# A ConvNeXt V2 block on one core: the normalised block on three of every four partitions, read in three parts, and written from ScalarE's queue

## The chip, the cores and the metric

The kernel runs on one core of a Trainium2 chip. The metric is the device time of one execution in microseconds; the comparison is between medians of several runs. A core has five engines that follow their own lists of instructions and meet only at semaphores: TensorE (PE, with weight loads shown apart as PEld), VectorE (DVE), ScalarE (ACT), GpSimd (POOL) and SyncE (SP), which here only issues DMAs. The data are moved by 16 DMA engines, which all queues share.

## The reference, cut to what matters

```python
def reference(x, dw, w1, w2, grn_gamma, grn_beta):      # x: (1, 512, 512, 96), bf16
    xp = jnp.pad(x, ((0,0),(1,1),(1,1),(0,0)))
    out = jnp.zeros_like(x)
    for i in range(3):
        for j in range(3):                               # depthwise 3x3
            out = out + xp[:, i:i+H, j:j+W, :] * dw[i, j]
    h = _layernorm(out, axis=-1)                         # over the 96 channels
    h = jnp.einsum('bhwc,ce->bhwe', h, w1)               # 96 -> 384
    h = _gelu(h)                                         # tanh approximation
    gx = jnp.sqrt((h * h).sum(axis=(1, 2), keepdims=True) + 1e-6)   # over all pixels
    nx = gx / (gx.mean(axis=-1, keepdims=True) + 1e-6)
    h = grn_gamma * (h * nx) + grn_beta + h
    h = jnp.einsum('bhwe,ec->bhwc', h, w2)               # 384 -> 96
    return x + h
```

The sum over all pixels in `gx` divides the work: nothing of the output can be made before every pixel has gone through the first product and the GELU.

## The kernel before

The image is cut into 128 blocks of GR = 4 rows (2048 pixels x 96 channels). There are two passes.

**First pass (to about 980 us).** A loop over slots `s` (L826 to L949) works as a software pipeline: in one slot, different blocks stand at different stages. A table `at`, made ahead of the loop (L794 to L820), says which block has which stage in which slot. For a block b in the usual case:

- x is loaded (SP) and turned by VectorE; PE makes the convolution in three bursts of matmuls; ScalarE copies the result to SBUF as `y_bf` (`evac`).
- POOL squares it (`ysq`, L512), PE sums `y_bf` and `ysq` over channels, and for every four blocks VectorE and POOL make the reciprocal standard deviations. They go through DRAM: `stage_rows` (L608) writes them as rows, `stage_bcast` (L626) reads them back as four broadcasts onto 32 partitions each, as `rbc`.
- POOL multiplies: `yn` = `y_bf` x `rbc` (`stage_norm`, L634), three buffers. The mean needs no step: the matrix w1 is centred instead (`setup_mlp`, L425).
- One slot later `stage_write` (L642) writes `yn` to `yn_dram` with four DMAs of 96 KB, one per row of the block (SBUF has four image rows of 32 channel groups on its 128 partitions; DRAM has one row per channel). One slot after that `stage_read` (L647) reads the block back as `ynT`, 96 channels on partitions 0 to 95, with one DMA of 384 KB, into a ring of six buffers. Partitions 96 to 127 of the ring were filled with zeros once (`setup_ynt`), and so were rows 96 to 127 of `w1p`, since the matmuls contract over 128 partitions.
- Two slots later the block has its "mlp" stage (`mlp_units`, L699): PE multiplies `ynT` and `w1p` into PSUM banks, and ScalarE makes the GELU, in nine activations: three over two banks (1024 columns), six over one (512). VectorE takes statistics of the result, or PE its Gram matrix. A third of the blocks ("whole") keep the GELU's result: it is stored to `g_dram` in three DMAs, one per slot (`store_next`).

In a slot with an mlp stage of a block below TAIL0 = 114 the order on ScalarE is: GELU over banks 0-1, GELU 2, GELU 3, GELU 4-5, GELU 6, GELU 7, `evac` of the convolution, GELU 8-9, GELU 10, GELU 11. Slots of the last 14 blocks have an order of their own (`mlp_tail`).

**Order on the queues.** Every engine call of the pass goes through a wrapper that keeps it in program order on its engine. On SP a slot issues in this order: the x load of block s + 4, the read, the four writes, the broadcasts, the rows, the store of `g`. ScalarE's queue issues six small loads at the start of the kernel and nothing afterwards.

**Completion semaphores.** The framework gives the DMAs issued from SP's and ScalarE's queues eight completion semaphores, in turn and in the order of the built program. A DMA is issued only when the one that used its semaphore before, the eighth before it, has landed. The program holds this wait as an instruction of the issuing queue, so it holds up what stands behind it there. POOL's DMAs have their own eight.

**Second pass (from about 980 us).** After the statistics have been joined and w2 scaled, the blocks are gone through once more, in an order `ORDER` that mixes those whose GELU was kept (5 in SBUF, 35 in `g_dram`, loaded by POOL's queue) with those that are made again (88). For these, `load_rest` (L283) reads `ynT` five blocks ahead: 85 blocks by one DMA of 128 rows (`yn_rows`, L125: the 96 channel rows of the block and 32 of the next one, 512 KB; rows 96 to 127 of `w1p` are zero), while three are still in the ring. PE multiplies again, ScalarE makes the GELU over 1536 columns (`gr`), PE multiplies by w2, VectorE adds `xb` (x plus bias, made by POOL from `xr`, which POOL's queue loads) into `o_sb` (four buffers), and SP stores it (`stage_out`, L350), 384 KB per block.

The prediction speaks of the functions shown here.

Of the kernel before, what the change touches and what calls it, by code (L numbers as in the profile page):

```python
# [12 lines left out]
GR = 4  # L13
# [43 lines left out]
def kernel(  # L57
# [11 lines left out]
    f32 = mybir.dt.float32  # L69
# [40 lines left out]
    def chans(i):  # L110
        return slice(i, 64, 2) if i < 2 else slice(64, 96)
# [8 lines left out]
        return flat_ap.rearrange("p (g r m) -> p g r m", r=GR, m=MB)  # L120

    def yn_src(q):
        return yn_dram[q].rearrange("c (r w) -> c r w", r=GR)

    def yn_rows(q):  # L125
        return yn_dram[q:q + 2].rearrange("q c (r w) -> (q c) r w", r=GR)[0:128]

    def yn_dst(q, r):
        return yn_dram[q].rearrange("(c i) (r w) -> r c i w", i=NI, r=GR)[r]
# [6 lines left out]
    dwx = consts.tile([9, NI, GR, 32], bf16, name="dwx")  # L136
    eye32 = consts.tile([128, 32], bf16, name="eye32")
    rowsel = consts.tile([128, GR], bf16, name="rowsel")
    w1_raw = consts.tile([C, E], bf16, name="w1_raw")
    w1p = consts.tile([128, E], bf16, name="w1p")  # L140
    Wq = consts.tile([128, NI, 3, GR, 32], bf16, name="Wq")
    w2_sb = consts.tile([128, NCH, C], bf16, name="w2_sb")
# [41 lines left out]
    with ExitStack() as p1:  # L184
# [66 lines left out]
        for q in range(GR):  # L251
            dve.tensor_copy(out=eye32[32 * q:32 * q + 32, :], in_=ident_f[32 * q:32 * q + 32, 32 * q:32 * q + 32])

        cen = consts.tile([C, 128], bf16, name="cen")
        xtpool = pc.enter_context(tc.tile_pool(name="xt", side="right", bufs=1))
        ypool = pc.enter_context(tc.tile_pool(name="ybf", side="right", bufs=13))
        ysqpool = pc.enter_context(tc.tile_pool(name="ysq", side="right", bufs=3))
# [25 lines left out]
        def load_rest(n, sq, pq):  # L283
            q = ORDER[n]
            v = grp.setdefault(q, {})
            if is_held(q):
                v["g"] = gs[q]
            elif is_whole(q):
                v["g"] = late.gl.tile([128, NQ, NCH, QW], bf16, name="gl")
                pq.dma_start(out=v["g"][:].rearrange("p t j w -> p (t j w)"), in_=g_dram[whole.index(q)])  # L290
            else:
                ynt = yn_ring[SLOTS[nth_made[q] % NYT]]
                if q not in KEPT:
                    sq.dma_start(out=ynt[:], in_=yn_rows(q))
                v["ynt"] = ynt

        def recompute(q, t):
# [87 lines left out]
        for j in range(GR):  # L385
            pool.memset(rowsel[32 * j:32 * j + 32, j:j + 1], 1.0)
        pool.memset(cen[:], 1.0)
        pool.memset(w1p[C:128, :], 0.0)
        dve.memset(SG, 0.0)
        busy(FILL[0])  # L390
        Ud = banks(2)[:, 0, :NI * 9].rearrange("p (i k) -> p i k", i=NI)
# [7 lines left out]
        n = 0  # L399
# [12 lines left out]
                            pool.tensor_copy(out=o, in_=i_)  # L412

        for i in range(NI):
            act.dma_start(out=w1_raw[i:C:NI, :], in_=w1[chans(i), :])
        act.dma_start(out=w2_sb[:], in_=w2.rearrange("(j p) c -> p j c", p=128))
        with nc.allow_non_contiguous_dma("tiny gamma/beta load"):
            act.dma_start(out=gam_bf[:], in_=grn_gamma.rearrange("(j p) -> p j", p=128))
# [1 line left out]

        def setup_ynt():
            for t in yn_ring:
                pool.memset(t[C:128, :, :].rearrange("p r w -> p (r w)").bitcast(f32), 0.0)

        def setup_mlp():  # L425
            Us = banks(1)[:, 0, :]
            w1m, b2_ps = Us[:, :E], Us[:, E:E + C]
            pe.matmul(w1m, lhsT=cen[:], rhs=w1_raw[:], start=True, stop=True)
            for j in range(NCH):
                pe.matmul(b2_ps, lhsT=bet_bf[:, j:j + 1].to_broadcast([128, 128]), rhs=w2_sb[:, j, :],  # L430
                          start=(j == 0), stop=(j == NCH - 1))
            dve.scalar_tensor_tensor(out=w1p[:C, :], in0=w1m[:C], scalar=-1.0 / C, in1=w1_raw[:],
                                     op0=ALU.mult, op1=ALU.add)
            dve.tensor_copy(out=B2bc_f[:], in_=b2_ps)

# [203 lines left out]
                               in1=rbcs[k][:, b - b0:b - b0 + 1, :].to_broadcast([128, NI, W]), op=ALU.mult)  # L639
            yns[b] = yn  # L640

        def stage_write(b):  # L642
            yn = yns.pop(b)
            for r in range(GR):
                sp.dma_start(out=yn_dst(b, r), in_=yn[32 * r:32 * r + 32, :, :])

        def stage_read(b):  # L647
            t = yn_ring[b % NYT]
            sp.dma_start(out=t[:C], in_=yn_src(b))
            ynts[b] = t  # L650

        bsts = {}
# [173 lines left out]
        for s in range(last_slot + 1):  # L826
            get = lambda kind: at.get((s, kind), [])
            if s + 4 < NBLK:
                load_x(s + 4)
            for b in get("read"):  # L830
                stage_read(b)
            for b in get("write"):
                stage_write(b)
            for k in get("bcast"):
                stage_bcast(k)
            for k in get("rows"):
                stage_rows(k)
            store_next()
            for k in get("newton"):
                stage_newton(k, pool)  # L840
            for b in get("norm"):
                stage_norm(b)
            for b in get("sqp"):
                stage_sq(b, False)
            for k in get("rstd"):
                stage_rstd(k, pool)
            mlp = get("mlp")

            def spread_out():
                for k in get("spread"):  # L850
                    stage_spread(k)
                for b in get("norma"):
                    stage_norm(b, dve if b < 2 else pool)

            spare = not mlp and s % 2 == 1
            taps, evac = conv_taps(s, spare) if s < NBLK else ([], None)
            if mlp and mlp[0] >= TAIL0:
                assert not taps
                square_owed()
                mlp_tail(mlp[0], get)  # L860
            elif not mlp:
                if s + 3 < NBLK:
                    turn_x(s + 3)
                for f in taps:
                    f()
                if not spare:
                    spread_out()
                if evac:
                    evac()
                for b in get("sqa"):  # L870
                    stage_sq(b, True)
                for b in get("stats"):
                    stage_stats(b)
                for k in get("moments"):
                    stage_moments(k)
                if spare:
                    spread_out()
                for k in get("chain"):
                    stage_moments(k)
                    stage_chain(k)  # L880
                for k in get("turn"):
                    stage_turn(k)
                gram_next(2)
                square_owed()
            else:
                b = mlp[0]
                unit, squares, squares_rest = mlp_units(b)
                conv = lambda n, fence=True: taps[n](fence) if taps else None

                conv(0)  # L890
                unit(0, 2)
                unit(2, 1)
                squares(0)
                conv(1, False)
                spread_out()
                if s + 3 < NBLK:
                    turn_x(s + 3)
                unit(3, 1)
                unit(4, 2)
                squares(1)  # L900
                gram_next(1 if taps else 2)
                unit(6, 1)
                squares(2)
                unit(7, 1)
                for k in get("turn"):
                    stage_turn(k)
                conv(2)
                if evac:
                    evac()
                gram_next(1 if taps else 2)  # L910
                unit(8, 2)
                unit(10, 1)
                for b2 in get("stats"):
                    stage_stats(b2)
                unit(11, 1)
                for k in get("moments"):
                    stage_moments(k)
                squares_rest(2)
                square_owed()
                if is_whole(b):  # L920
                    owed.append(lambda f=squares_rest: f(3))
                grams.extend((b, c) for c in range(cm_quads(b) * QC, NQ * QC, 2 * E))
                if is_whole(b):
                    stores.extend((b, h) for h in range(3))
            if s == 0:
                setup_ynt()
            if s == 3:
                setup_mlp()
            if s == 4:
                setup_rest()  # L930
            for b in get("combine"):
# [120 lines left out]
```

## Time and profile before

| What | Value |
|---|---|
| Runs | 1480.27, 1486.15 and 1486.81 us; median 1486.15 |
| Profiled execution | span 1480.8 us from the first to the last instruction; granted TensorE clock 0.994 |
| Busy share of the span | ACT 96%, PE 94%, POOL 88%, DVE 80%, PEld 55% |
| DMA | 433 MB moved, 292 GB/s on average; SP's queue 326 MB, POOL's 103 MB |
| Writes of yn | 512 DMAs of 96 KB |
| Reads of ynT | 128 DMAs of 384 KB (first pass), 85 of 512 KB (second pass) |
| Stores of the output | 127 DMAs of 384 KB and 4 of 96 KB |

The time of the profiled execution is not listed beside its span; the span lies at the lower end of the runs. Busy times are sums over instructions, and an instruction that issues a DMA or waits for a semaphore is not counted as busy (on POOL, whose own cores prepare its DMAs, it is). The profile shows each wait with the engine or DMA that ended it; where a wait is for several things, it names the one that came last, and the names of DMAs in it can be off where several share a semaphore.

### The profile page before, as it was taken

How to read it: one execution, taken by the hardware profiler on the slowest of the kernel's cores; microseconds unless marked ns; L12 is line 12 of the kernel's file. 1: busy time of each engine (PE TensorE's matmuls, PEld its weight loads, DVE VectorE, ACT ScalarE, POOL GpSimd, SP SyncE). 2: the span in 40 equal slices, each digit the busy share in tenths (PEclk: the TensorE clock that was granted, in tenths of full speed). 3: DMA queues.
4: the chain of work that ended last, by engine and by line, in shares of the span. 5: the costliest groups of instructions: out<-in, count | busy, mean ns of one | idle time of the engine just before them, and what ended most of it. 6: DMA issues, size and time to landing. Idle time of an engine off the chain costs nothing.

```text
span 1480.8 us, 54225 instructions
## 1 busy us (share of the span) xinstructions
PE 1391.3 (94%) x23125; PEld 810.4 (55%) x23125; DVE 1182.0 (80%) x2135; ACT 1414.4 (96%) x1595; POOL 1300.3 (88%) x922
## 2 busy tenths in 40 slices
PE   8888999999999999999999997789999999999998
PEld 3434444444444444444444445467777777776776
DVE  7849989999999999999999987965555555555555
ACT  7888989999999999999999999999999999999997
POOL 3459889998998999998999987569999999999997
PEclk9999999999999999999999999999999999999999
DMA  5568788788888888888888866669999999999997
GB/s 180 179 205 255 241 253 280 228 271 260 260 248 264 258 264 255 276 253 254 263 258 266 263 216 195 195 225 409 366 359 402 417 416 413 419 410 417 411 412 282
DMA packets 167768, 433.08 MB, mean 292 GB/s; under 512 B 31558, under 2 KB 81318, under 8 KB 163046
## 3 DMA queue, kind: packets, MB, share of 16 engines
q1 hardware_dynamic: 151284, 326.04, 66.3%
q0 software_dynamic: 14880, 103.43, 17.6%
q8 instruction: 181, 2.97, 0.8%
q14 instruction: 61, 0.50, 0.1%
q10 hardware_dynamic: 1362, 0.15, 0.1%
HBM read 273.30 MB, written 156.22 MB: 290 GB/s over the span
## 4 chain that ended last, share of the span: by engine, by line
PE 30%; ACT 24%; DMA 19%; POOL 13%; DVE 6%; issue 4%; SPq 4%; POOLq 0%; ACTq 0%; DVEq 0%
PE PS L35 30%; ACT g L35 16%; DMA out_dram<-o_sb 9%; POOL yn L35 6%; ACT y_bf L35 5%; POOL ysq L35 5%; SPq L35 4%; DMA yn_dram<-yn 3%; DVE bst L35 3%; DMA xin<-in_x_dram 2%; DMA rbc<-r_dram 2%; DMA ynT<-yn_dram 1%; DMA g_dram<-g 1%; DVE o_sb L35 1%; ACT xT L35 1%
## 5 line engine op out<-in xcount | busy, mean ns | idle before, releaser
L35 ACT ACTIVATE g<-PS 128x512 bf16<-128x512 f32 (+2 forms) x1062 | 727.7, 864 | 16.5 <-PE PS L35 15.6
L35 DVE BATCH_NORM_STATS2 bst<-g 128x6 f32<-128x512 bf16 x1110 | 671.3, 672 | 35.4 <-ACT g L35 34.5
L35 PE MATMUL PS<-ynT,w1p 128*128 128x512 bf16 x2181 | 609.6, 381 | 23.6 <-ACT g L35 5.4
L35 ACT ACTIVATE gr<-PS 128x1536 bf16<-128x1536 f32 x360 | 498.5, 1459 | 18.8 <-PE PS L35 13.8
L35 POOL TENSOR_TENSOR yn<-y_bf,rbc 128x1536 bf16<-128x1536 bf16 x126 | 391.3, 3108 | 77.3 <-ACT rbc L35 21.9
L35 DVE TENSOR_TENSOR o_sb<-PS,xb 128x384 bf16<-128x384 f32 x512 | 277.3, 556 | 227.0 <-PE PS L35 190.1
L324 POOL TENSOR_TENSOR xb<-xr,B2c 128x1536 f32<-128x1536 bf16 x118 | 368.1, 3133 | 4.3 <-DVE o_sb L35 2.0
L35 PE MATMUL PS<-xT,Wq 64*32 64x511 bf16 (+1 forms) x9198 | 340.5, 389 | 26.2 <-ACT y_bf L35 8.1
L35 POOL TENSOR_TENSOR ysq<-y_bf 128x1536 bf16<-128x1536 bf16 x114 | 313.6, 2752 | 12.8 <-ACT y_bf L35 12.8
L35 PEld LDWEIGHTS <-w1p 128*128 128x128 bf16 x2181 | 171.6, 98 | 222.0 <-issue 133.4
L35 PEld LDWEIGHTS <-gr 128*128 128x128 bf16 x4296 | 212.1, 98 | 68.9 <-issue 12.0
L35 PE MATMUL PS<-W2s,gr 128*128 128x96 bf16 x4224 | 223.5, 206 | 8.2 <-DVE o_sb L35 8.0
L35 PEld LDWEIGHTS <-Wq 64*32 64x32 bf16 x9216 | 111.9, 90 | 193.3 <-issue 145.9
L35 ACT ACTIVATE y_bf<-PS 128x1536 bf16<-128x1536 f32 (+2 forms) x135 | 199.4, 1482 | 17.4 <-PE PS L35 13.3
L35 DVE STREAM_TRANSPOSE xT<-xin 128x576 f32<-128x576 f32 (+1 forms) x256 | 181.4, 748 | 8.1 <-DMA xin<-in_x_dram 8.1
L35 PEld LDWEIGHTS <-g 128*128 128x128 bf16 x1704 | 104.9, 98 | 86.3 <-issue 54.3
L35 PE MATMUL PS<-w1p,ynT 128*128 128x256 bf16 (+2 forms) x822 | 125.8, 273 | 8.0 <-ACT xT L35 3.2
L35 PE MATMUL PS<-g 128*128 128x128 bf16 x1464 | 122.6, 220 | 2.9 <-DVE PS L35 2.6
L35 PEld LDWEIGHTS <-gl 128*128 128x128 bf16 x1680 | 82.8, 98 | 26.8 <-issue 5.0
L35 PE MATMUL PS<-W2s,gl 128*128 128x96 bf16 x1680 | 89.5, 206 | 3.4 <-DVE o_sb L35 3.2
L35 PEld LDWEIGHTS <-ynT 128*128 128x128 bf16 x822 | 64.1, 97 | 31.5 <-issue 13.7
L279 POOL DMA_DIRECT2D xr<-in_x_dram x115 | 63.7, 555 | 14.2 <-POOL xb L324 14.2
(105 smaller groups left out, 576.5 us busy)
## 6 DMA issues: line engine op xcount, KB each, us to landing
xin<-in_x_dram SPq DMA_DIRECT2D x126, 432.0 KB
g_dram<-g SPq DMA_DIRECT2D x105, 512.0 KB
gl<-g_dram POOLq DMA_DIRECT2D x35, 1536.0 KB, 11.3
yn_dram<-yn SPq DMA_DIRECT2D x512, 96.0 KB
ynT<-yn_dram SPq DMA_DIRECT2D x128, 384.0 KB
out_dram<-o_sb SPq DMA_DIRECT2D x127, 384.0 KB
xr<-in_x_dram POOLq DMA_DIRECT2D x123, 384.0 KB, 6.9
ynT<-yn_dram SPq DMA_DIRECT2D x85, 512.0 KB
```

Source lines behind the costliest of these rows:

```text
L35: r = f(*a, **k)
L279: pq.dma_start(out=xr[:], in_=x[0, r0:r0 + GR].rearrange("r w c -> (r w) c").rearrange("(p g) c -> p g c", g=PXP))
L324: pq.tensor_tensor(out=xb[:], in0=grp[q]["xr"][:], in1=bias[:, None, :].to_broadcast([128, PXP, C]), op=ALU.add)
```

## The change

`yn` in `ynT` no longer lies on partitions 0 to 95 but on three of every four of all 128 partitions: DRAM row 3c + i goes to partition 4c + i for i = 0, 1, 2, and partitions 3, 7, 11 and so on stay zero. The rows of w1 are laid out in the same way, with zeros between (`w1_raw` is filled with zeros before its loads, on POOL, and `w1p` and the matrix `cen` of ones take all 128 partitions). One block is read by three DMAs of 32 rows (128 KB each) with a partition step of four, in both passes; the second pass no longer reads rows of the next block.

In "steady" slots, those with an mlp stage of a block below TAIL0, the four writes are issued from ScalarE's queue instead of SP's: after GELU 0-1, after GELU 4-5, after `evac` and after GELU 8-9. SP's order in these slots is x load, broadcasts, rows, store, and then the three parts of the read. Other slots keep their order and SP's queue. In the built program 440 writes (110 blocks) stand on ScalarE's queue, and the DMAs on the two queues go from 1291 to 1717.

```diff
     def yn_src(q):
-        return yn_dram[q].rearrange("c (r w) -> c r w", r=GR)
-
-    def yn_rows(q):
-        return yn_dram[q:q + 2].rearrange("q c (r w) -> (q c) r w", r=GR)[0:128]
+        return yn_dram[q].rearrange("(c i) (r w) -> i c r w", i=NI, r=GR)
+
+    def read_yn(eng, t, q):
+        for i in range(NI):
+            eng.dma_start(out=t[i:128:4], in_=yn_src(q)[i])
...
-    w1_raw = consts.tile([C, E], bf16, name="w1_raw")
+    w1_raw = consts.tile([128, E], bf16, name="w1_raw")
...
                 if q not in KEPT:
-                    sq.dma_start(out=ynt[:], in_=yn_rows(q))
+                    read_yn(sq, ynt, q)
...
-        pool.memset(w1p[C:128, :], 0.0)
+        pool.memset(w1_raw[:], 0.0)
...
-            act.dma_start(out=w1_raw[i:C:NI, :], in_=w1[chans(i), :])
+            act.dma_start(out=w1_raw[i:128:4, :], in_=w1[chans(i), :])
...
-                pool.memset(t[C:128, :, :].rearrange("p r w -> p (r w)").bitcast(f32), 0.0)
+                pool.memset(t[:].rearrange("p r w -> p (r w)").bitcast(f32), 0.0)
...
-        def stage_write(b):
+        def write_parts(b, eng):
             yn = yns.pop(b)
-            for r in range(GR):
-                sp.dma_start(out=yn_dst(b, r), in_=yn[32 * r:32 * r + 32, :, :])
+            return [lambda r=r: eng.dma_start(out=yn_dst(b, r), in_=yn[32 * r:32 * r + 32, :, :]) for r in range(GR)]
 
         def stage_read(b):
             t = yn_ring[b % NYT]
-            sp.dma_start(out=t[:C], in_=yn_src(b))
+            read_yn(sp, t, b)
...
-            for b in get("read"):
-                stage_read(b)
-            for b in get("write"):
-                stage_write(b)
+            mlp = get("mlp")
+            steady = bool(mlp) and mlp[0] < TAIL0
+            wparts = [f for b in get("write") for f in write_parts(b, act if steady else sp)]
+            if not steady:
+                for b in get("read"):
+                    stage_read(b)
+                while wparts:
+                    wparts.pop(0)()
             for k in get("bcast"):
                 stage_bcast(k)
             for k in get("rows"):
                 stage_rows(k)
             store_next()
+            if steady:
+                for b in get("read"):
+                    stage_read(b)
+
+            def write_next(n=1):
+                for f in wparts[:n]:
+                    f()
+                del wparts[:n]
...
                 unit(0, 2)
+                write_next()
                 unit(2, 1)
...
                 unit(4, 2)
+                write_next()
                 squares(1)
...
                 if evac:
                     evac()
+                write_next()
                 gram_next(1 if taps else 2)
                 unit(8, 2)
+                write_next(len(wparts))
                 unit(10, 1)
```

More of the change, by code (lines that the diff above doesn't have):

```diff
@@ L252 @@
             dve.tensor_copy(out=eye32[32 * q:32 * q + 32, :], in_=ident_f[32 * q:32 * q + 32, 32 * q:32 * q + 32])
-        cen = consts.tile([C, 128], bf16, name="cen")
+        cen = consts.tile([128, 128], bf16, name="cen")
         xtpool = pc.enter_context(tc.tile_pool(name="xt", side="right", bufs=1))
@@ L431, in setup_mlp @@
                           start=(j == 0), stop=(j == NCH - 1))
-            dve.scalar_tensor_tensor(out=w1p[:C, :], in0=w1m[:C], scalar=-1.0 / C, in1=w1_raw[:],
+            dve.scalar_tensor_tensor(out=w1p[:], in0=w1m, scalar=-1.0 / C, in1=w1_raw[:],
                                      op0=ALU.mult, op1=ALU.add)
@@ L846 @@
                 stage_rstd(k, pool)
-            mlp = get("mlp")
             def spread_out():
```

## The prediction

> **What bounds the kernel now.** I read the table by stretch first, because the first 900 us (the pipelined pass) and the last 500 us (the output pass) have different limits. Its columns are busy time of PE, PEld, DVE, ACT and POOL, granted clock, DMA share and GB/s.
>
> ```profile
> 200.00:860.00 660.00, 632.32 (x11431) 309.18 (x11429) 652.70 (x1119) 655.82 (x932) 616.66 (x462) 1.00 0.83 259
> 860.00:985.00 125.00, 103.22 (x1190) 63.19 (x1189) 99.72 (x199) 119.34 (x108) 82.60 (x54) 0.99 0.63 198
> 985.00:1475.00 490.00, 478.60 (x7000) 354.93 (x6998) 270.00 (x499) 470.41 (x340) 467.91 (x278) 1.00 1.00 396
> ```
>
> In the steady stretch ScalarE works 655.8 of 660 us, so nothing that leaves ScalarE's list alone can gain more than the 4.2 us it idles there; what is added to its queue may cost in full. In the output pass the DMA engines are full (share 1.00), but PE, ACT and POOL are each above 95% too.
>
> Next, ScalarE's own timeline at the start: the only place where it issues DMAs today (ACTq is its sequencer).
>
> ```profile
> 5.42 0.44 ACT L35 ACTIVATE Wq<-g 32x288 bf16<-32x288 bf16 x1 [1.46 <-DVE g L35]
> 5.59 0.59 ACTq L35 DMA_DIRECT2D w_raw<-in_w_dram  x1
> 5.77 0.88 ACT L35 ACTIVATE Wq<-g 32x288 bf16<-32x288 bf16 x2
> 6.23 0.59 ACTq L35 DMA_DIRECT2D w_raw<-in_w_dram  x1
> 8.15 0.49 ACTq L35 DMA_DIRECT2D gam_bf<-in_grn_gamma_dram  x1
> 11.63 0.38 ACTq L35 DMA_DIRECT2D bet_bf<-in_grn_beta_dram  x1
> 12.06 1.45 ACT L35 ACTIVATE y_bf<-PS 128x1536 bf16<-128x1536 f32 x1 [4.16 <-DMA gam_bf<-in_grn_gamma_dram]
> ```
>
> Two things are seen. The first load is issued (5.59) while five copies written ahead of it still run back to back until 7.89: an issue of 0.6 us runs beside activations already handed over. And an issue that must wait holds everything behind it: the load at 11.63 waited for the completion semaphore it shares with an x load, which by the trace's semaphore records landed at 11.61; the convolution result could be copied only at 12.06, after 4.16 us idle.
>
> Third, what ScalarE's few idle microseconds in the steady stretch come from: SP's queue around 670 us, POOL's timeline, then ScalarE's.
>
> ```profile
> 665.81 4.37 SPq L35 DMA_DIRECT2D yn_dram<-yn  x4
> 670.23 1.99 SPq L35 DMA_DIRECT2D rbc<-r_dram  x4
> ```
> ```profile
> 677.33 3.11 POOL L35 TENSOR_TENSOR yn<-y_bf,rbc 128x1536 bf16<-128x1536 bf16 x1 [3.22 <-DMA xin<-in_x_dram]
> ```
> ```profile
> 696.17 1.51 ACT L35 ACTIVATE g<-PS 128x1024 bf16<-128x1024 f32 x2 [1.37 <-PE PS L35]
> 698.55 2.49 ACT L35 ACTIVATE g<-PS 128x512 bf16<-128x512 f32 x4 [0.87 <-PE PS L35]
> ```
>
> The row broadcasts (rbc) stand behind four yn writes; POOL, nearly full itself, stands 3.22 us (I take the wait to be for rbc, which it reads), its squares come late, PE's statistics wait, and ScalarE idles. From the first GELU of block 16 (192.6) to that of block 114 (887.6) are 98 slots, 695.0 us; the usual slot is 7.03, so such hiccups cost 695.0 - 688.9 = 6.1 us (the 4.2 above are the part of it from 200 to 860).
>
> Last, the output pass: the chain from 980 us on by line, and the waits from 1000 to 1450.
>
> ```profile
> by line: PE PS L35 68.9%; DMA out_dram<-o_sb 26.9%; DVE o_sb L35 3.1%; issue 0.4%; DVEq L35 0.1%
> ```
> ```profile
> DVE o_sb L35 <- DMA out_dram<-o_sb: 34.6, 23, 2.7
> POOL xr L279 <- POOL xb L324: 14.2, 48, 0.3
> PE PS L35 <- DVE o_sb L35: 10.9, 13, 1.6
> ```
>
> Output stores land late, so DVE waits for an o_sb buffer and PE for DVE: 10.9 us. But POOL, from 980.1 to 1472.5, waits for another engine only some 4 us (its 14.2 us are waits for itself).
>
> **The change, part by part.**
>
> *Writes move to ScalarE.* 110 blocks x 4 = 440 issues. On SP one takes 0.60 us (median); on ScalarE's queue the loads above took 0.59. Within a slot (starts read from the one at 333.87) the activations start at 0.00, 0.92, 1.40, 1.87, 2.78, 3.25, 3.73 (the copy of the convolution), 5.06, 5.97 and 6.44. Each write stands behind a long activation, whose successor starts 0.91 to 1.33 us later. PE's result is ready about 0.1 us before the first GELU starts, so the worst case is the first write: 0.05 + 0.60 against 0.92 leaves 0.27 us. Taken: nothing, covered by the running activation. If the cover failed wholly: 440 x 0.6 = 264 us; below nothing is excluded, since no work leaves ScalarE. One issue in twenty on SP took over about 1.2 us (0.3 beyond the cover), 440 x 5% x 0.3 = 6 us at most; 1 taken, as ScalarE's queue is empty where SP's was not.
>
> The Trainium skill, "Perfetto Trace Analysis", section on the per-instruction lifecycle, says that an issue from either of these queues first locks one shared descriptor generator. By it a first write could stand behind one read's issue (0.33 us), and 0.98 against 0.92 would cost 98 x 0.06 = 6 us. The trace shows no such lock: at 0.74 us both queues issue together, SP in 0.40 us as it does alone later.
>
> *What the writes wait for.* The first waits for POOL's normalised block. Today in one slot of four it ends up to 2.7 us (once 3.9) after the slot's first GELU, which hides 0.3; but when ScalarE slips once, POOL is no longer late. Bounds 0 and +4 us; taken 0, because the broadcasts no longer stand behind four writes, 4.4 us in the rows above, and POOL starts that much sooner.
>
> All four wait for a completion semaphore: eight are used in turn by SP's and ScalarE's DMAs, so each write waits until the eighth DMA before it has landed. In 23 of the steady slots (about one in four) the built order makes that, for the third write, the first part of the read that SP issues only when the previous slot's fourth write has landed. The loop: the fourth write's issue ends 4.65 to 5.66 into its slot; it lands 2.80 later (median of fourth writes, 200 to 860 us, semaphore records); read issue 0.33; landing 3.0 (the nearest row: broadcasts of 32 rows of 4 KB). That is 10.8 to 11.8, or 3.8 to 4.8 into the next slot, while the third write must start by 5.06 - 0.60 = 4.46. So 0 to 0.3 us of stall: 23 x 0.1 = 2.3 us taken. With medians over all writes and whole reads (3.22 and 4.59) the loop is 2.0 longer: 23 x 2.3 = 53 us. I take the short rows since the writes leave the queue in which they stood behind 384 and 432 KB, and a part is a third of a read. Behind a stalled write stand the GELUs, then PE (its banks), DVE and all.
>
> *SP.* Per steady slot it loses four issues (2.4 us) and gains two (0.66); reads land some 11 us before their use today, and the later writes take some 3 of these. The broadcasts no longer queue behind writes: of the 6.1 us of hiccups I take 4 back, of ScalarE's 5.7 us idle from 860 to 985 (POOL waits there 10.0 us for rbc) 2. In the ramp reads keep their place and two on the chain get 0.66 longer: +1.3.
>
> *Output pass.* 85 reads shrink from 512 to 384 KB: 11 MB of 194 (490 us at 396 GB/s), 5.7%. DMA is then no longer full, stores land sooner, PE's 10.9 us could go. What is late next is POOL, which can finish only about 4 us earlier: -3.5 taken. Bounds: -4 by POOL; above, see the third rival. POOL's fills of the read buffers, now of 128 partitions, keep their length per partition (5.41 us for six) and end at 12.2, before the first read at 25.8; that of w1_raw takes the place of w1p's, 0.42 us that end at 2.8, before its loads at 5.59. Both cost nothing.
>
> Sum against the profiled execution (its own time is not listed beside its span): +1 +0 +2.3 -4 -2 +1.3 -3.5 = -4.9 us; the span of 1480.8 becomes 1475.9. That span lies 5.35 below the median of the three runs, so 1481 on their scale.
>
> **Rivals.**
>
> *A. Writes hidden, small sum* (likeliest): 1481, with the bounds of its small terms 1474 to 1491. For it: the overlap at the start.
>
> *B. Slower: the write-read-write loop.* Place: third write in one slot of four. Price 0.6 to 2.3 us each, 14 to 53 in all: 1493 to 1532. It stalls from where the landings of write and read part together pass 6.0 us and decides from 6.6 (nearest rows 5.8, the long ones 7.8). Against it: a slower slot unloads the DMAs and shortens the loop.
>
> *C. Slower: ScalarE pays for issues*, as the sequencer may not hand the next GELU over in time: 0.1 to 0.3 us per write, +44 to +132: 1525 to 1610. Against it: 5.59 above.
>
> *D. Output pass chokes on eight semaphores.* DMAs per block go from 1.66 to 2.99 at 3.85 us per block, so the eighth before was issued 10.3 us ago rather than 18.5; today's stores land after 10.5 (median), reads after 11.4. With today's landings 58% of issues would wait, 0.7 us at the median, 3.4 at the ninth decile. Price 0 to +20, and the 3.5 not gained: 1485 to 1505. Against it: fewer bytes in flight land sooner.
>
> *E. Faster throughout:* hiccups (6.1), 860-985 (5.7) and POOL's 4 all come back, no stall: -16, 1470.
>
> *The change does nothing to traffic:* no; the 128 KB less per read is in the access pattern.
>
> **How the numbers follow.** A 0.45, E 0.15, B 0.22, C 0.08, D 0.10. A measurement here tells about 0.5%, 7.4 us: 1478.7 and 1493.6. Faster: E and four tenths of A, 0.33. Slower: C, B, half of D: 0.35. Same: the rest, 0.32. Range 1470 (E) to 1525 (B without its end): C, B's end and half of E stay outside, 2 in 10; A alone has 1474 to 1491.
>
> **What would show it.** Right: ScalarE's slots stay at 7.03 us with ACTq issues of 0.6 us beside activations; no wait of "ACT g" for a yn, read or rbc DMA; POOL's waits for rbc gone; DMA share in the output pass near 0.95, DVE's 34.6 us for stores smaller, POOL the engine without gaps. Wrong: gaps on ScalarE after the copy of the convolution in every fourth slot (B), gaps after every write (C), SP waiting for its own reads after 985 us (D).

## The result and the profile after

The changed kernel takes 1580.53 us (median, 1575.65 to 1591.38) against 1483.32 us of the kernel before in the same session: ratio 1.0654, 95% interval 1.062 to 1.0687. It is 97 us slower where 1481 was forecast, and outside the range.

The table by stretch of the changed kernel, with the columns of the prediction's first fence. The first two stretches are those shown of before; the third is as long as the old third one and lies in the output pass.

```profile
200.00:860.00 660.00, 581.79 (x10117) 281.17 (x10116) 585.02 (x991) 591.40 (x825) 555.68 (x418) 0.96 0.78 232
860.00:985.00 125.00, 113.33 (x1941) 56.41 (x1941) 109.95 (x188) 115.65 (x160) 108.09 (x82) 0.95 0.74 222
1085.00:1575.00 490.00, 480.49 (x7035) 356.75 (x7032) 272.46 (x503) 469.84 (x340) 467.24 (x278) 1.00 0.98 376
```

In the steady stretch ScalarE works 591.4 of 660 us instead of 655.8: 68.6 us idle against 4.2. No engine has taken its place as the bound, and the DMA engines move less per second (232 against 259 GB/s). The granted clock of the steady stretch fell from 1.00 to 0.96, and PE's matmuls of 512 columns over `ynT` went from 382 to 398 ns; with PE busy for 581.8 of 660 us this is not the bound, but what share it has in the loss was not separated. (The kernels with one write per block, below, have a clock of 1.00 again.) From the first GELU of block 16 to that of block 114 the time goes from 695.0 to 781.2 us: these 98 slots hold 86 us of the loss. The ramp ahead of them adds 6.0, the slots from there to block 122 some 2.5. From block 122 to the end nothing changes (525.1 and 525.0).

ScalarE's timeline from the end of one slot through a bad slot (492.79 to 502.42; lines of the activations in between left out), then SP's queue in the same time:

```profile
491.18 0.58 ACTq L35 DMA_DIRECT2D yn_dram<-yn  x1
492.87 0.56 ACTq L35 DMA_DIRECT2D yn_dram<-yn  x1
493.71 2.00 ACT L35 ACTIVATE g<-PS 128x512 bf16<-128x512 f32 x3
496.28 0.56 ACTq L35 DMA_DIRECT2D yn_dram<-yn  x1
496.88 1.09 ACT L35 ACTIVATE g<-PS 128x512 bf16<-128x512 f32 x2 [1.17 <-DMA xin<-in_x_dram]
497.85 1.46 ACT L35 ACTIVATE y_bf<-PS 128x1536 bf16<-128x1536 f32 x1
499.64 0.56 ACTq L35 DMA_DIRECT2D yn_dram<-yn  x1
500.24 1.02 ACT L35 ACTIVATE g<-PS 128x1024 bf16<-128x1024 f32 x1 [0.93 <-DMA ynT<-yn_dram]
```
```profile
490.84 0.53 SPq L35 DMA_DIRECT2D xin<-in_x_dram  x1
491.47 0.38 SPq L35 DMA_DIRECT2D g_dram<-g  x1
496.79 1.73 SPq L35 DMA_DIRECT2D ynT<-yn_dram  x3
```

This is ScalarE's part of the loss in small. The second write of the slot stands until 496.28: it takes over the semaphore of the x load issued at 490.84, which by the semaphore records landed at 496.26. Meanwhile SP stands from 491.85 to 496.79, because its read may only follow the landing of the fourth write of the slot before, issued at 491.18 and landed, by the semaphore records, at 496.67. The third write then takes over the semaphore of that read's first part, issued at 496.79 and landed at 499.62, and is issued at 499.64; the GELU behind it starts 0.93 us late. Each queue waits for the other's landings.

The waits of the changed kernel, of ScalarE, POOL and SP's queue (engine, what it waited for, us, times, longest):

```profile
ACT g L35 <- PE PS L35: 39.0, 59, 1.9
ACT g L35 <- DMA ynT<-yn_dram: 31.1, 21, 2.7
POOL yn L35 <- DMA yn_dram<-yn: 62.2, 30, 4.6
```
```profile
SPq L35 <- DMA yn_dram<-yn: 351.5, 139, 7.4
```

I matched each write on ScalarE's queue in the trace with the DMA whose semaphore it takes over, and took ScalarE's idle time right behind it. Writes that were issued as their semaphore came free, by what held it:

| Place of the write | Held by | Times | Idle behind it, us |
|---|---|---|---|
| second | x load | 21 | 8.3 |
| second | rows | 13 | 3.2 |
| third | part of a read | 23 | 26.5 |
| fourth | part of a read | 35 | 10.5 |
| fourth | store of g | 15 | 10.5 |
| first | none; POOL's yn was late | 4 | 5.8 |

With smaller ones that is 70 us: most of what ScalarE idles in these slots. The other 304 writes, whose semaphore was free, cost 0.9 us together.

In the output pass DVE's waits for stores have gone (35.4 us before), and it waits for POOL instead. The waits of the changed kernel from 1095 to 1545:

```profile
DVE o_sb L35 <- POOL xb L325: 47.5, 57, 2.1
PE PS L35 <- DVE o_sb L35: 5.6, 15, 1.0
DVE o_sb L35 <- DMA out_dram<-o_sb: 0.7, 1, 0.7
```

### The profile page after: what moved, and what is told of

Read it like the earlier page. It is cut to its first block, busy times and chain, and to the rows that moved or that the text cites. A ratio compares the mean times of both kernels' runs of the same rounds, so it can differ in the third digit from the quotient of the medians.

```text
span 1575.6 us, 54824 instructions
## 1 busy us (share of the span) xinstructions
PE 1417.7 (90%) x23125; PEld 819.7 (52%) x23125; DVE 1196.8 (76%) x2135; ACT 1429.7 (91%) x1595; POOL 1300.7 (83%) x922
## 5 line engine op out<-in xcount | busy, mean ns | idle before, releaser
L35 DVE BATCH_NORM_STATS2 bst<-g 128x6 f32<-128x512 bf16 x1110 | 679.3, 673 | 123.4 <-ACT g L35 122.9
L35 PE MATMUL PS<-ynT,w1p 128*128 128x512 bf16 x2181 | 625.2, 387 | 97.4 <-ACT g L35 66.4
L35 PE MATMUL PS<-xT,Wq 64*32 64x511 bf16 (+1 forms) x9198 | 349.1, 398 | 30.6 <-ACT y_bf L35 15.1
L35 PEld LDWEIGHTS <-w1p 128*128 128x128 bf16 x2181 | 176.2, 98 | 278.5 <-issue 179.1
L35 ACT ACTIVATE y_bf<-PS 128x1536 bf16<-128x1536 f32 (+2 forms) x135 | 191.0, 1420 | 17.1 <-PE PS L35 12.8
```

The costliest lines, as they stand in the source:

```text
L35: r = f(*a, **k)
```

## The experiments

Theories: **T1**, ScalarE's queue stands at writes through the shared semaphores. **T2**, an issue itself costs ScalarE time. **T3**, the three-part read as such is slow. **T4** and **T6**, SP's new order does it. **T5** (SP's loop of writing a block, waiting for it to land and reading it is too long) and **T8** (SP has too many DMAs) were formed on the way. The ratios are to the kernel before, measured beside each run, with 95% intervals.

### The three parts of the change, one by one

Three switches: L, the layout with three-part reads; O, SP's new order; A, the writes on ScalarE. The changed kernel is L+O+A.

Writes back on SP (L+O):

```diff
-            wparts = [f for b in get("write") for f in write_parts(b, act if steady else sp)]
+            wparts = [f for b in get("write") for f in write_parts(b, sp)]
...
+                while wparts:
+                    wparts.pop(0)()
```

> Everything of the change is kept (three-part reads, their place behind the store in SP's list), except that SP issues the four writes, at the end of its list for the slot. T1 (ScalarE's queue stands at a write until the eighth DMA before it has landed, and SP's next reads stand until the fourth write has landed): ScalarE's queue holds no DMA any more, so the 86 us of the steady slots go almost wholly, slots of 7.03 us, 1475 to 1495 us. T2 (an issue itself costs ScalarE time, 440 times): the same 1475 to 1495. T3 (the three-part reads cost the time, by their own issues on SP and their small packets): stays within 20 us of 1580. T4 (the new order on SP makes POOL and the GELUs late): stays within 20 us of 1580. So this run parts T1 and T2 from T3 and T4.

Old layout and whole reads, writes on ScalarE, new order (O+A). Against the changed kernel (not shown: `yn_src`, w1 and the reads of the second pass are as before, too):

```diff
-            read_yn(sp, t, b)
+            sp.dma_start(out=t[:C], in_=yn_src(b))
...
```

> The layout of before (one read of 96 partitions per block), but the writes from ScalarE's queue at the four places and SP's order as in the changed kernel. Per steady slot 8.5 DMAs instead of 10.5, so a write waits for a DMA issued 8/8.5 = 0.94 slots (6.6 us) earlier instead of 8/10.5 = 0.76 slots (5.4 us). T1: most of the loss goes, but not all, since whole reads land later than parts: 1490 to 1550 us. T2 (price of the issue itself, same 440 issues): stays within 15 us of 1580. T3 (three-part reads): 1475 to 1495, all gone.

Layout alone (L):

```diff
-            steady = bool(mlp) and mlp[0] < TAIL0
+            steady = False
```

> Three-part reads alone: SP's old order (x load, read, writes, broadcasts, rows, store), writes on SP throughout. T5 (SP's own loop: four writes issued, their landing, then the reads they release, and only then the next four writes): before, from the blocks of 300 to 900 us, 2.80 + 2.86 + 0.52 wait + 0.44 = 6.6 us, under the slot of 7.03; three parts take 2.0 instead of 0.44, 8.2 with the old landing, 7.7 with the one of the first experiment (whose slots were 7.66). So SP becomes the bound: 98 slots x 0.6 to 1.1 us = +59 to +108, 1540 to 1590, PE waiting for the reads' landing. T1 (ScalarE's queue alone is to blame): 1475 to 1490.

Order alone (O): the reads and then the four writes stand behind the store, all else as before.

> The old layout and whole reads, writes on SP; only SP's order in the steady slots is new (broadcasts, rows, store, then read, then writes). T5: the loop keeps its 6.6 us, so nothing of size changes: 1475 to 1490. T6 (the order itself is to blame, as the reads stand behind the store and the broadcasts): 1510 to 1560.

Layout and writes on ScalarE, old order (L+A); and writes on ScalarE alone (A), which is the same edit on O+A:

```diff
+            for b in get("read"):
+                stage_read(b)
             for k in get("bcast"):
...
-            if steady:
-                for b in get("read"):
-                    stage_read(b)
```

> The changed kernel with SP's reads put back ahead of the broadcasts; writes on ScalarE, three-part reads. T1 (completion semaphores, eight for all of SP's and ScalarE's DMAs): still 10.5 DMAs per slot, so ScalarE still stands at its writes: 1555 to 1600. T6 (the new order of the reads): 1500 to 1550.

> Writes on ScalarE alone: the old layout and SP's old order, the four writes at the places of the changed kernel. T1: 8.5 DMAs per slot; as in the second experiment (1545) ScalarE stands at writes whose eighth DMA before has not landed: 1520 to 1560. T6 or T5 alone (order, or SP's loop, as the only causes): 1475 to 1495, since both are undone.

| Parts | Median, us | Ratio | Interval |
|---|---|---|---|
| O | 1477.73 | 0.9948 | 0.992 to 0.9977 |
| L | 1547.63 | 1.043 | 1.0368 to 1.0491 |
| L+O | 1548.87 | 1.0441 | 1.0399 to 1.0482 |
| A | 1545.62 | 1.0419 | 1.0365 to 1.0473 |
| O+A | 1544.53 | 1.0412 | 1.0361 to 1.0462 |
| L+A | 1583.01 | 1.0667 | 1.0613 to 1.0721 |
| L+O+A | 1580.53 | 1.0654 | 1.062 to 1.0687 |

The first run met no theory's number: taking the writes off ScalarE gives back only a third. With the others the picture is plain. The order costs nothing and gains half a per cent (T4 and T6 fall). Layout and queue each cost 4% alone, and 6.5% together. So there are two causes, each enough by itself to lose 4%.

### Cause one: SP's queue is too full for three-part reads

With L alone nothing is on ScalarE's queue, yet ScalarE is idle for 41.6 of the 660 us. Waits of that kernel from 200 to 860:

```profile
POOL yn L35 <- DMA rbc<-r_dram: 39.3, 13, 6.4
ACT g L35 <- PE PS L35: 38.4, 34, 2.2
PE PS L35 <- POOL ysq L35: 31.2, 19, 3.2
```

Before, these three were 4.0, 3.2 and 3.4 us. (The DMA's name can be off: with POOL's waits put down to loads of x and stores of g, 20.8 us before and 49.2 now.) SP issues the broadcasts late, POOL gets them late, squares late, PE's statistics and then ScalarE follow. The question was whether SP is late because its loop of writes, landing and reads is too long (T5), or because of the number of its DMAs. Two tiny loads per block (into a small tile of their own), between the read and the writes and, in a second kernel, behind the writes:

```diff
             for b in get("read"):
                 stage_read(b)
+            for i in range(2 * len(get("read"))):
+                sp.dma_start(out=tiny[32 * i:32 * i + 32, :], in_=w1[32 * i:32 * i + 32, :16])
```

> The kernel before (whole reads, writes on SP) with two tiny loads (1 KB each) per block on SP's queue, between the read and the four writes: the two extra issues of the three-part read, without its parts. T5 (SP's loop of write issue, landing, read issue): the loop of 6.6 us grows by 2 x 0.6 and passes 7.03: +40 to +75, 1523 to 1560. T3 (three parts cost by their small packets or landings): 1480 to 1492.

> The same two tiny loads, behind the four writes, where SP issues while the writes land (its wait there is the cover): the same number of DMAs per slot (10.5) and of issues on SP, but outside the loop. T5: 1480 to 1505, at least 25 us below the kernel with the loads between read and writes. T1's count of DMAs (a semaphore every eighth DMA) or SP's sheer issue time as the cause on SP too: the same time as that kernel, within 10 us.

They took 1533.96 us (1.0343, 1.03 to 1.0387) and 1541.49 us (1.0406, 1.036 to 1.0451). Two loads of 1 KB cost almost what the three-part reads cost, so no bytes are needed for such a loss (T3), and they cost it at either place: for these loads T5, a loop in which only the place between read and writes counts, is refuted. What counts is how many DMAs SP has to pass in a slot. Then fewer must undo it: one write of 128 partitions per block in place of four, with the layout kept and its rows in DRAM in the order of the partitions:

```diff
-            return [lambda r=r: eng.dma_start(out=yn_dst(b, r), in_=yn[32 * r:32 * r + 32, :, :]) for r in range(GR)]
+            return [lambda: eng.dma_start(out=yn_dram[b].rearrange("c x -> (c x)").rearrange(
+                "(p i w) -> p i w", p=128, i=NI), in_=yn[:])]
...
-        return yn_dram[q].rearrange("(c i) (r w) -> i c r w", i=NI, r=GR)
+        return yn_dram[q].rearrange("c x -> (c x)").rearrange("(r c i w) -> i c r w", r=GR, i=NI, w=W)
```

> Three-part reads alone with SP's old order (the fifth experiment, 1548), but each block written with one DMA of 128 partitions (its rows in DRAM in the order of the partitions) instead of four of 32: 7.5 DMAs per slot on SP instead of 10.5. The parts then read in pieces of 1 KB instead of 4 KB. T8 (number of DMAs on SP, by their issue and by the eight semaphores): SP's 6.8 us of issues and steps per slot become about 4.8, slots of 7.03 us, GELU to GELU of blocks 16 and 114 690 to 700; 1478 to 1505 in all, the upper end if the small pieces cost in the output pass. T3 (three parts as such): slots stay at 7.5, 1540 to 1580.

Measured 1471.82 us, ratio 0.9909 (0.9878 to 0.994): 76 us below the same kernel with four writes, and faster than before. Its steady stretch, in the columns above, and SP's queue over one slot:

```profile
200.00:860.00 660.00, 627.74 (x11457) 312.06 (x11454) 655.13 (x1124) 659.80 (x934) 620.68 (x465) 1.00 0.78 260
```
```profile
508.29 2.75 SPq L35 DMA_DIRECT2D ynT<-yn_dram  x3
511.14 0.54 SPq L35 DMA_DIRECT2D yn_dram<-yn  x1
513.57 1.15 SPq L35 DMA_DIRECT2D r_dram<-rt  x2
514.82 0.42 SPq L35 DMA_DIRECT2D g_dram<-g  x1
515.60 0.34 SPq L35 DMA_DIRECT2D xin<-in_x_dram  x1
```

ScalarE is full (659.8 of 660), and SP's list has holes. The parts now read pieces of 1 KB, and the time after block 122 is not longer for it (521.4). What the spread layout itself is worth here is open: one write with the old layout was not tried. SP's 700 us from 200 to 900, from its issues and the semaphore records:

| Kernel (writes on SP) | DMAs per slot | Issuing | Steps between issues | Standing |
|---|---|---|---|---|
| before | 8.5 | 482 | 39 | 179 |
| L | 10.5 | 581 | 49 | 69 |
| two tiny loads in front of the writes | 10.5 | 529 | 42 | 126 |
| two tiny loads behind the writes | 10.5 | 536 | 45 | 118 |
| L with one write | 7.5 | 424 | 38 | 239 |

Before, 50 of the 179 us were waits for POOL's yn: SP was ahead. With L these are 8; it issues most of the time, and 52 of the 69 us that it still stands are reads waiting for the block just written to land. So for L itself the loop of T5 is not excluded: its sum had 1540 to 1590, and joining the writes shortens the loop as well as the list. With the tiny loads (0.42 and 0.58 us to issue) some 60 us each are waits of stores, broadcasts, rows and x loads for the semaphore of the eighth DMA before (11 before the change), and the waits for POOL's yn are 4 and 17. In all three SP's lead over POOL is gone or nearly so. What an issue costs by its time and what by its turn at a semaphore was not separated. The Trainium skill, "DMA: Bandwidth & Descriptors", rules for kernel authors, advises to coalesce many small transfers and calls those under 64 KB mostly overhead. Here four writes of 96 KB were still worth joining (1547.6 to 1471.8 us), for their number on the queue: the bytes stayed the same.

In the changed kernel this first cause does not act in the same form: with the writes on ScalarE, SP issues for only 320 of these 700 us and stands for 353, of which 258 are waits for writes to land. How the parts lift the loss there from 4.1% to 6.5% was not separated; they raise the DMAs per slot from 8.5 to 10.5, so that each takes over its semaphore from a more recent one.

### Cause two: ScalarE's queue and the shared semaphores

Each read one slot later, so that it no longer waits for a write issued just before:

```diff
-                put(s + 2, "read", b)
+                put(s + (2 if ramp else 3), "read", b)
```

> The changed kernel with each read one slot later in the steady slots, so that SP's reads no longer wait for a write issued late in the slot just before. T1: if the loop write, read, write makes the loss, SP's 351 us of waits for the writes' landings go and the third and fourth writes' waits for read parts (37 of the some 70 us attributed to writes) with them; what stays are waits for x loads, rows and stores: 1490 to 1530 us. T2 and T3: within 15 us of 1580, as issues, DMAs and their sizes are the same.

Four tiny loads more per slot:

```diff
+                for i in range(4):
+                    sp.dma_start(out=tiny[32 * i:32 * i + 32, :], in_=w1[32 * (i % 3):32 * (i % 3) + 32, :16])
```

> The changed kernel with four tiny loads (32 x 16, 1 KB each) added to SP's list in every steady slot, after the reads. 14.5 DMAs per slot instead of 10.5: a write waits for a DMA issued 8/14.5 = 0.55 slots (3.9 us) earlier instead of 5.4 us, while landings take 2.5 to 4.6 us. T1: markedly slower than the changed kernel, by 40 to 250 us: 1620 to 1830. T2 and T3: ScalarE's list and the reads are unchanged, SP has room for four more issues (2.4 us of its idle time): 1575 to 1600.

No reads in the steady slots:

```diff
                 for b in get("read"):
-                    stage_read(b)
+                    ynts[b] = yn_ring[b % NYT]
```

> The changed kernel without the reads of the steady slots (the MLP of those blocks works on old data; everything else is issued as in the changed kernel, all 440 writes from ScalarE's queue among it). 7.5 DMAs per slot, so a write waits for a DMA issued 8/7.5 slots = 7.5 us earlier, while landings take 2 to 5 us; and no read stands between one write and another. T1 (semaphores): most of the 97 us go, 1485 to 1515. T2 (the issue itself costs ScalarE): 1540 to 1580, since it has the same issues.

One write per block on ScalarE's queue, and the same write on SP's:

> The changed kernel (ScalarE's queue, three-part reads behind the store) with one write of 128 partitions per block, at the first of the four places; 7.5 DMAs per slot, 110 writes on ScalarE. T1 (ScalarE's queue waits for SP's DMAs through the shared semaphores, and SP's for ScalarE's): one place per slot at which it can stand instead of four; in the run without steady reads the first write cost 25 stalls of 1 us: 1475 to 1510, slower than the same write on SP by 5 to 35. T2 (issue time on ScalarE): a quarter of 440 issues, about a quarter of the loss: 1490 to 1505. If ScalarE's queue costs nothing once the DMAs are few: equal to the same write on SP within 5.

> The same with the one write per block on SP, behind the reads: the layout and the order of the change, 7.5 DMAs per slot, nothing on ScalarE's queue. T8 (number of DMAs on SP's queue): slots of 7.03 us as in the run with one write and the old order (1472); the new order was worth 3 us in the steady slots with the old layout: 1464 to 1476.

| Kernel | Median, us | Ratio | Interval |
|---|---|---|---|
| change, reads a slot later | 1608.81 | 1.0839 | 1.0794 to 1.0884 |
| change, four tiny loads more | 1620.94 | 1.095 | 1.089 to 1.101 |
| change, no steady reads | 1561.6 | 1.0513 | 1.0453 to 1.0572 |
| change, one write, on ScalarE | 1474.82 | 0.9933 | 0.9908 to 0.9958 |
| change, one write, on SP | 1472.17 | 0.992 | 0.9888 to 0.9952 |

The first two speak for semaphores and against issue time: ScalarE's issues are the same in both, and both are slower than the change. But I had expected the later reads to help. There ScalarE's fourth writes waited for x loads instead (26 times, 52.3 us) and its first ones for rows (24 times, 21.8): with the reads moved, another DMA is the eighth before.

The run without reads missed my number too. It has 7.5 DMAs per slot, and I had expected the stalls to go; its time alone would have fitted T2. Its waits do not. Of ScalarE, from 200 to 860:

```profile
ACT g L35 <- PE PS L35: 24.3, 37, 1.2
ACT g L35 <- DMA rbc<-r_dram: 17.3, 10, 2.7
```

By the semaphore records 25 first writes waited for rows (24.4 us) and 44 third and fourth ones for broadcasts (29.9 us), while 359 writes whose semaphore was free cost 0.1 us. The rows that held ScalarE up land 1.39 us after their issue, but SP issued them only 1.9 us (median) before ScalarE fell idle. SP was not late with them: their own semaphore had been free for 6.9 us or more, and they were issued within 0.05 us of VectorE finishing the tile that they carry (`rt`). For this tile SP stood 222 of its 700 us, for semaphores of earlier DMAs 200 (40 of these for ScalarE's writes). So a count of DMAs does not give the price. What counts is which DMA a write takes over from, and how late that one is issued, be it for a third engine's work.

The last pair settles T2. With one write at one place ScalarE does not stand:

```profile
508.12 1.51 ACT L35 ACTIVATE y_bf<-PS 128x1536 bf16<-128x1536 f32 x1
509.45 3.04 ACT L35 ACTIVATE g<-PS 128x1024 bf16<-128x1024 f32 x4
511.54 0.33 ACTq L35 DMA_DIRECT2D yn_dram<-yn  x1
512.38 2.98 ACT L35 ACTIVATE g<-PS 128x512 bf16<-128x512 f32 x5
```

One of its 110 writes waited (2.6 us). The 110 issues cost nothing that can be measured: 1474.8 and 1472.2, with intervals that overlap. T2 had 1490 to 1505. The Trainium skill, "DMA: Bandwidth & Descriptors", section on issuing engines that are not separate DMA queues, says that issuing from several engines only saves the sequencer time of the issue. That holds for one write. For four, the runs show what it leaves out: a queue that also carries GELUs paid 4.2%.

### The output pass

The traffic that the change saves there, without parts:

```diff
-                    sq.dma_start(out=ynt[:], in_=yn_rows(q))
+                    sq.dma_start(out=ynt[:C], in_=yn_src(q))
```

> The kernel before, only with the output pass reading 96 rows instead of 128, still in one DMA: the traffic that the change saves, without parts or moved writes. If POOL sets the output pass (per group 3.13 for the addition, 0.55 for issuing the load of x, 34/118 x 0.54 for issuing a load of g, 0.12 waits: 3.96, and the additions follow each other every 3.96 us before, 3.95 in the changed kernel): no change, 1480 to 1487, though DVE's 35 us of waits for stores go. If the full DMA engines set it: -10 to -28, 1458 to 1476.

The same with the order O and the loads of x on SP's queue:

> The order of the sixth experiment (1478), 96 rows in one read in the output pass, and the loads of x of that pass issued from SP's queue instead of POOL's: POOL's 3.96 us per group become 3.4. If POOL sets the output pass: PE is next (busy 390.7 of 400 us), a group 3.87 us, 115 x 0.09 = -10: 1463 to 1472. If not, or if SP's eight semaphores bind there (2.7 DMAs per group, the eighth before issued 11.5 us ago, landings 6 to 11): 1475 to 1495.

Every fourth addition on VectorE, on the kernel with the order alone and on the changed kernel:

```diff
-                stage_xb(ORDER[n + 2], pq, B2c)
+                stage_xb(ORDER[n + 2], dve if n % 4 == 3 else pq, B2c)
```

> The sixth experiment's kernel (new order alone, 1478) with every fourth addition of the output pass on VectorE instead of GpSimd. GpSimd's 3.96 us per group become 3.2, VectorE's 2.2 become about 3. If GpSimd sets the output pass even with reads of 512 KB: PE is next at 3.87, -10: 1463 to 1472. If the full DMA engines (share 1.02, 410 GB/s) set it too: 1473 to 1484.

> The changed kernel with every fourth addition of the output pass on VectorE. Only the output pass counts here: its additions follow each other every 3.95 us, GpSimd's own 3.96. If GpSimd sets it now that the reads are 384 KB: 3.87 per group, 1568 to 1575 in all. If not: 3.95, 1577 to 1585.

All four were slower than any theory had it. In this order they took 1507.64 us (ratio 1.0157, 1.0124 to 1.0189), 1510.15 (1.0178, 1.0141 to 1.0216), 1489.26 (1.0021, 0.9992 to 1.005) and 1606.56 (1.0804, 1.0744 to 1.0863). Reading 96 rows to partitions 0 to 95 saves a quarter of these reads' bytes and costs 21 us after block 122 (545.8 against 525.1). The DMAs from 1120 to 1400, of before and of that kernel:

```profile
DMA packets 25834, 115.69 MB, mean 413 GB/s; under 512 B 3364, under 2 KB 3364, under 8 KB 22972
```
```profile
DMA packets 23007, 103.48 MB, mean 370 GB/s; under 512 B 3185, under 2 KB 3185, under 8 KB 20325
```

The DMA engines are as busy as before (share 1.02 in both) and move a tenth less. The changed kernel reads the same 384 KB to three of every four partitions and does not lose it (525.0). The spread over partitions may be the reason; it is not shown, as the two also differ in the number of DMAs. The second kernel has the same 96-row reads (553.6 us after block 122), so it tells nothing clean about POOL.

The additions on VectorE were meant to show that POOL is the bound. They took 1.85 us there instead of 3.13, but POOL got new waits; from 1150 to 1400 in the changed kernel with this edit:

```profile
POOL xb L325 <- DVE o_sb L35: 24.7, 16, 2.2
POOL xr L280 <- DVE xb L35: 17.9, 16, 1.6
```

So whether POOL alone sets the output pass stays open. For it speaks the changed kernel's chain of waits from 1075 on: 61.2% is POOL's additions and 8.2% its issues of x loads, where before PE and the stores stood.

## Why the prediction was wrong

- **Issues hidden beside activations (+1):** right. 304 writes with a free semaphore cost 0.9 us, and 110 in the last pair nothing.
- **The shared descriptor generator** that the prediction weighed: ScalarE's writes took 0.56 us to issue in the median, both the 278 that an issue of SP's overlapped (ninth decile 0.58) and the 162 others (0.56). No lock is seen in these numbers.
- **First write's wait for POOL (0, at most +4):** 5.8 us in four slots. Over 5 of these lie in two slots in which POOL itself had stood 9.4 and 10.1 us for its broadcasts (rbc), so "POOL starts that much sooner" did not hold there.
- **Loop stall of the third write (+2.3): the step that failed first.** The mechanism was named, and the 23 pairings of third write and read part were right, but they cost 26.5 us, 1.15 each where 0.1 was taken, within the 0 to 2.3 each between the short and the long rows. The short rows summed landing, read issue and landing to 6.1 us (2.80, 0.33 and 3.0). Where the third write was held, it was 7.2 in the median: the fourth write landed after 4.7, the part was issued 0.13 later and in 0.45, and landed after 1.9. So the landing of the fourth write was mis-sized: "since the writes leave the queue in which they stood" did not make it short (4.2 us in the median of all fourth writes). And the fourth write was issued later in its slot (its issue ended at 6.35, not 4.65 to 5.66), as writes ahead of it had stood. The larger miss: only this pairing was priced. The other three writes have an eighth DMA before them too, and x loads (4.2 us to land), stores (4.6), rows and read parts held them: another 38 us. "A slower slot unloads the DMAs and shortens the loop", which stood against rival B, did not come true.
- **SP: "loses four issues and gains two (0.66)": the second step that failed.** A part took 0.59 us to issue (median), no less than a write, although a whole read takes 0.32; about +1.4 per slot where 0.66 was taken. More important, SP's standing time was taken for room. It is the cover behind which landings hide, and L alone, at 4.3%, shows that it was used up. In the changed kernel SP issues less than before, but it stands 351 us, over the whole kernel, for writes to land (133.5 before).
- **Hiccups back (-4 and -2):** right in size for the order alone: -0.5%; in its profiled execution, the slowest of its ten (1487.31), the steady slots went from 695.0 to 691.7 and those from block 114 to 122 from 68.2 to 65.4. The changed kernel did not get them: there POOL waits 25.0 us for rbc from 200 to 860 (4.0 before).
- **Ramp (+1.3):** +6.0, which says little: block 16 began at 194.2, 196.2 and 202.2 us in three kernels with the same first pass (O).
- **Output pass (-3.5):** 0.0. DVE's waits for stores went and POOL came next, as written; what POOL could still finish earlier was not gained. Rival D's choking on eight semaphores did not come: DVE waited 0.7 us for a store.

Rival B had the mechanism right and one of its places: 26.5 us, within its price of 14 to 53. The other three places and SP's own queue, which costs 4.3% with no write on ScalarE, were in no rival. The span of rival C (1525 to 1610) holds the measured time only by luck: the runs refute its mechanism. Of the signs listed as "wrong", gaps after the copy of the convolution are there, and so are others.

## What to carry to other kernels

Count the DMAs per stage on every queue that shares a ring of completion semaphores, and for each DMA on a compute engine's queue name the DMA whose semaphore it takes over, when that one can be issued at the latest, on which engine's work it waits itself, and how long it takes to land. All places have to be priced, not the one that catches the eye. A queue's standing time is cover: splitting one transfer in three cost 4% while its bytes stayed the same, and joining four writes in one gave it all back, and made both the layout and the move harmless.

## What was not expected of the hardware

- A DMA of 32 rows with a partition step of four took 0.59 us to issue in the median (0.45 the first of three, 0.59 the others) and one of 96 rows 0.32 us, although it carries a third of the bytes; in the output pass, where ScalarE's queue issues nothing, it was the same. Why is not shown.
- 256 loads of 1 KB on SP's queue cost 50 to 58 us, though they move almost no data.
- Reads of 96 rows onto partitions 0 to 95 kept the DMA engines as busy as reads of 128 rows and moved a tenth less.
